# Block-recurrent cross attention and mixture of depths on one core: transfers held behind a fetch of rows, score rows by TensorE, and reads in 32x64 tiles

## The chip, the core and the metric

The kernel runs on one core of a Trainium2 chip. A core has TensorE (PE, with its weight loads, PEld), VectorE (DVE), ScalarE (ACT), GpSimd (POOL) and SyncE (SP), and 16 DMA engines which carry what SP, ACT and POOL issue. Times are microseconds on the device. The time before is 209.79, the median of three runs (207.62 to 210.34).

## What is computed

Two blocks, one after the other, all in float32. The first is attention in both directions between x (8 batches, 8 heads, 512 rows, 64 columns) and a state (32 rows in each head). The second takes from each batch of 544 rows (512 of x, 32 of the state) the 128 with the highest score and sends these through a two-layer network; all other rows pass unchanged.

```python
scores = scale * np.matmul(x, state.transpose(0, 1, 3, 2))     # softmax over the 32 state rows
xread = np.matmul(a, state)
scores2 = scale * np.matmul(state, x.transpose(0, 1, 3, 2))    # softmax over the 512 rows of x
sread = np.matmul(a2, x)
...
scores = np.einsum('bsd,d->bs', x, w_gate)       # x: now (8, 544, 512)
for b in range(B):
    top_idx = np.argpartition(-scores[b], capacity)[:capacity]   # capacity 128
    h = np.maximum(x[b, top_idx] @ w1, 0.0)      # w1: 512 x 1024
    ye = h @ w2                                  # w2: 1024 x 512
    g = 1.0 / (1.0 + np.exp(-scores[b, top_idx]))
    out[b, top_idx] = x[b, top_idx] + g[:, None] * ye
```

## The kernel before

The work is cut into 676 pieces. Each piece belongs to one engine, has a name and a batch, and knows which pieces must come before it. They are numbered as the program makes them, and the list ORDER says in which order they are emitted; each engine then runs its own pieces strictly in that order. In `30/6/w08` the piece is 30, its PSUM bank is 6, and `w08` puts 8 warm-up matmuls (L159) that write bank 0 ahead of it.

A batch runs through these pieces:

- `load_x` (L284): the 1 MB of x of the batch, in two or four transfers. For batches 4 to 7 `load_x2` (L299) brings a second, rearranged copy in four transfers of 256 KB, which VectorE turns in blocks (`blocks`, L395); for batches 0 to 3 TensorE turns x (`turn`, L391).
- `scores` (L428): state against x on TensorE. VectorE makes the softmax over the state in passes over 128 x 1024 elements: `in` (L447), `max` (L458), `sub` (L461), `sum` (L468), `mult` (L473), `out` (L476). ScalarE takes the exponentials. The softmax over x goes by `smax` (L482) and `sexp` (L486).
- `read` (L539): two pieces a batch, on TensorE. The weights are 32 rows of the softmax, 128 columns wide, and the moving operand is the state with one more column, in which the gate is already multiplied in, so that the read leaves the scores of the 512 rows as well (`gate`, L547). With `b in WIDE` a read is 16 matmuls in tiles of 32x128. The rows are copied out by ScalarE (`rows`, L543).
- `sread` (L601): the read of x for the state, on TensorE. Batches 4 to 7 turn its weights through DRAM (`a_out`, L567, and `a_in`, L572).
- `store_x` and `store_s` (L631, L635): all 544 rows of the batch to the output in DRAM, for batches 0 and 1 from ScalarE's queue, for the others from SP's.
- The choice. Each row must be compared with all others, so the 544 scores are laid out as one row on all 128 partitions. Batches 0 to 3 do this on TensorE, by four transposes of a broadcast column and a fifth for the state's rows (`row`, L673, and `row_s`, L676), with two copies by ScalarE. Batches 4 to 7 (`ROWS_OUT`) turn the scores once (`row_t`, L681), write them to DRAM from ScalarE's queue (`row_out`) and read them back on all partitions from SP's (`row_in`, L688). VectorE compares in five windows (`win`, L708), TensorE counts (`over`, L734), VectorE makes a one-hot table (`oh`, L745), TensorE picks row numbers and scores with it (`pick`, L761), and VectorE adds up the row number (`index`, L765).
- `fetch` (L770): GpSimd brings the 128 chosen rows back from the output in DRAM by an indirect transfer. It waits for the stores of its batch.
- The two layers, for the batches in the groups [0], [1, 2], [3, 4], [5, 6], [7]: `xg` (L827) turns the fetched rows, `first` (L868) is 8 pieces, `second` (L888) 4 pieces a batch (or two halves of 4, `second_h`, in batches 6 and 7), then `add` and `put`, which writes the rows back by number.

Five buffers take x and the states, so x of batch 4 takes the place of the states, and x of 5 that of batch 0. There is one buffer for the rearranged copy: x2 of the next batch waits for `blocks` of the last.

Of the kernel before, what the change touches and what calls it, by code (L numbers as in the profile page):

```python
# [18 lines left out]
0 1 4 2 17 3 6 7 8 9 19 30/6/w08 26/5 32/0 10 11 34/4 36/7 18 33 37 12 113/3 5 27 35 31 13 14 38/0 115/6 24/5 117/2 39  # L19
118 25 116 114 15 40/0 28/7 16 44 41 119/5 22 21 23 20 29 45 120 46 42 53 178/2 62/6 180/3 182/5 64/7 184/4 121/0 43  # L20
183 179 65 63 185 267/7 66/5 268 181 67 47 48 126 122 70 49/2 51/4 269/3 50 52 270 127 128 271/4 71/7 174/2 141/6
143/5 175 142 272 144 54/0 176/6 145/4 273/5 123 132 124 55 487 72 125 56 57 146 177 274 129 149 58/0 150/7 328/6
485/4 61 130 151 59 131 73/5 75/7 329 60 68 74 76 486 133/0/w01 137/4 135 136 139 140 69 330 81 78 80 134 77 79 138
186/2 83/4 152/5 154/6 275/0 82 147 148 153 155 191 84 187 85 157 192 193 86/6/w43 206/7 88 280 159 156 158 160 188 89
161 208/3 87 207 209 281 282 210/5/w23 295/4 162/6 163 164 189 297/2 95/6 165/3/w31 296 298 166 96 190 299/7 276 194
167 195 197 196 90 169 97/6 98 102/4 99 103 100 198/0 277 278 104 211 170 101 200 91 201 279 105 286 214 199 202/0
215/6 106 205 204 283 216 203 284 285 333 336 331 332 335 422 423 213 334 488 489 212 587 92 168 226 107/5 217/0 219/2
300 218 220 223 225 221 222 224 108 239/6 287/0 227/4 109 240 289 290 340 337 228 288 229 93 230/7 303 232 291/0 110
304/6 233 94 338 339 292 111 305 231 293 294 424 301 425 171 315 234 112 341/1 241/6 306/5 308/4 342 346 343 242 307
309 347 235 348 236 314 344 361 352 362 426 363 302 427 345 349 312 350 313 351 311 429 431 430 428 252/6 253 243/4  # L30
249/5 246/7 244 353/0 250 247 310 354 245 355 356 254 248 251 364 490 316/4 357/0 365/6 317 172 318 358 359 360 366
492 367 432/4 319/3 369 370/7 433 237 371 321 434 437 261/6 372/0 255/7 262 256 263 257 258 373 374 320 438 439 435
452 173 322 238 323 381 453 493 375 454 368 491 436 455 440 441 376 378 380 379 377 442 382/5 444/0 446 447 495 383
384 445 394/5 385/4 264 448/0 387 259 494 496 443 497 388 589 590 456/7 386 395 450 451 324 457 265 449 460 498/4
396/6 461/3 462 503 463/2 397 464 465 504 505 260 325 389 472 407/7 404/2 401/6 398/3 408 399 405 402 518 519 499 500
501 591 520 466 592 521 458 459 502 390 400 406 403 506 471 507 470 469 467 468 508 473/5 510/0 509 593 474 511 475
522/4 476/5 391 512 513 523 409 326 594 392 478 526 514/0 527/6 410/7 515 595 528 596 516 517 327 479 538 529/4 530
531 597/2 598 602 599 603 604 477 524 532 617 618 600 534 537 535 533 536 525 619 588 601 605 620 411 416/4 412 413
417 539/6 540 541 606 418 542/5 544 608 607 414 551/6 419 609/0 621/7 611 543 612 622 552 545 480 546 610 625 553/5
613/0 626/7 614 627 628/7 547 554 616 629 630 615 481 624 631 623 637 393 548 266 482 636 483 420 632 635 634 633  # L40
558/5 564/6 555/1 561/2 559 562 556 565 557 560 563 638/5 566 639 640 567/4 568 641/5 581/1 569 570 574/7 582 583 643
549 642 421 484 415 550 644 645 646 573 647 650/3 575 576 584 577 651 578 585 571 648 657/5 658 659 652/4 653 654 655
660 579 580 649 586 662 572 669 656 661 663/4/w03 670/2 664 671 665 666 672 673 667 674 668 675
# [4 lines left out]
def kernel(  # L48
# [10 lines left out]
    nc = tc.nc  # L59
# [32 lines left out]
    TURNED = (0,)  # L92
    GATES_PE = (0, 2)
    WIDE = (0, 1, 2, 3, 4, 5, 6, 7)
    ROWS_OUT = (4, 5, 6, 7)
# [177 lines left out]

    def load_x(b, pieces=2):
        buf = xf[b] = Buf(R_X)
        n = H // pieces
        p_x[b] = []
        for h in range(0, H, n):

            on = "ACT" if b == 0 and h + n == H else "SP"  # L280

            def go(h=h, on=on):
                queue = nc.scalar if on == "ACT" else nc.sync
                queue.dma_start(out=buf.ap[:, h:h + n], in_=x[b, h:h + n].rearrange("h (p c) d -> p h c d", c=NC))  # L284

            chain = [q for q in last_load if q.engine == on][-1:]
            p_x[b].append(add(on, "load_x", go, after=chain, takes=[] if h else [buf], uses=[buf] if h else [], b=b))
            last_load.append(p_x[b][-1])

    def load_x2(b):  # L290

        buf = x2[b] = Buf(R_X2)
        p_x2[b] = []
        for w in range(2):
            for e in range(2):
                def go(w=w, e=e):
                    src = x[b].rearrange("h (s t r w) (e d) -> w e t r h s d", s=4, t=32, r=2, e=2)[w, e]
                    o = 32 * (2 * w + e)
                    nc.sync.dma_start(out=buf.ap[o:o + 32], in_=src)  # L299

                p_x2[b].append(add("SP", "load_x2", go, after=[p_scores[b - 2]], takes=[] if p_x2[b] else [buf], uses=[buf] if p_x2[b] else [], b=b))
# [316 lines left out]
    def touches(b, st, by_number=False):  # L618
        for bb, others in touch.items():
            if bb != b:  # L620
                for s, n in others:
                    if n or by_number:
                        tc.declare_no_dep(st.ins, s.ins, reason="rows of another batch")
        touch.setdefault(b, []).append((st, by_number))

    def store_base(b, xs, tmp, p_xs, p_xt):
        on = "ACT" if b < 2 else "SP"
        queue = nc.scalar if on == "ACT" else nc.sync

        def x_rows():  # L630
            touches(b, queue.dma_start(out=out[b, 0:S].rearrange("(p c) m -> p c m", c=NC), in_=xs.ap))  # L631

        def s_rows():
            dst = out[b, S:SP].rearrange("n (g q d) -> q n g d", g=2, q=4)
            touches(b, queue.dma_start(out=dst, in_=tmp["xt"]))  # L635

        return [add(on, "store_x", x_rows, after=p_xs, uses=[xs], b=b), add(on, "store_s", s_rows, after=[p_xt], b=b)]

    def by_number(b, **kw):

        touches(b, nc.gpsimd.indirect_dma_start(**kw), True)  # L641
        nc.gpsimd.memset(z1, 0.0)

# [3 lines left out]
    def choice(b, tmp, p_sc, p_xt, p_st1):  # L647
# [105 lines left out]
        for lo, hi in slot_tiles:  # L753
# [16 lines left out]
            def fetch(m=m, u=u, xr=xr):  # L770
                by_number(b, out=xr.ap[0:m], out_offset=None, in_=flat_out[0:SP * (b + 1)],
                          in_offset=bass.IndirectOffsetOnAxis(ap=u["idx"].ap[0:m, 0:1], axis=0))
# [31 lines left out]
            u["got"] = add("POOL", "fetch", fetch, after=[p] + p_st1, takes=[xr], uses=[u["idx"]], b=b)  # L804
            q = add("POOL", "below", below, after=[q], takes=[u["z"]], uses=[u["ax"]], b=b)
# [159 lines left out]
```

## Time and profile before

| | |
|---|---|
| median of three runs | 209.79 |
| the profiled execution's own time | 207.89 |
| its span, first to last instruction | 206.1 |
| mean granted TensorE clock | 0.963 |
| DMA | 36.14 MB, mean 175 GB/s |
| fetches of rows, issued at | 40.99, 58.54, 69.25, 95.28, 110.24, 133.39, 149.48, 174.53 |
| issue to landing of the eight, least, median, most | 3.3, 3.9, 5.6 |
| last matmul starts, last put starts | 198.7, 202.10 |

A group of instructions in the timeline is a start, a duration, an engine, a line, what is written from what, and a count; in square brackets stands the idle time ahead of it and what ended it. A matmul of float32 appears as two instructions. The chain of waits is the work that ended last, followed back from the end. A row by window gives the busy time of PE, PEld, DVE, ACT and POOL, then the granted clock (1.00 is full), the busy share of the DMA engines and what they moved.

### The profile page before, as it was taken

The page shows a single profiled execution, that of the slowest core. Times are in us where ns is not written, and L with a number is a line of the kernel's source. Part 1 is how long each engine was busy: PE and PEld are TensorE (multiplying, and loading weights), DVE is VectorE, ACT ScalarE, POOL GpSimd, SP SyncE. Part 2 cuts the span into 40 slices and gives each one's busy share as a digit, 9 for nine tenths or more (in the row PEclk, how much of TensorE's full clock was granted, in tenths as well). Part 3 has the DMA queues.
Part 4 walks back from the last instruction along what each step waited for, and adds up shares of the span by engine and source line. Part 5 has one row for each costly group of instructions (what it writes and reads, how often), then busy time and mean ns, then how long its engine had stood idle before and what let it go on. Part 6 is the DMA issues. An engine that isn't in the chain of part 4 may idle for free.

```text
span 206.1 us, 5307 instructions
## 1 busy us (share of the span) xinstructions
PE 192.1 (93%) x2204; PEld 141.5 (69%) x2204; DVE 125.6 (61%) x293; ACT 75.7 (37%) x174; POOL 49.3 (24%) x147
## 2 busy tenths in 40 slices
PE   7999997979999999999989999999999999999960
PEld 3786775558976568884456788844578885699840
DVE  2379896696959699848988579769940511011010
ACT  2399984463274252163305522524052040010200
POOL 7030010071032260014304300120064231305222
PEclk9999997596999999999999999999999999999995
DMA  6999999992399199988586999465833520100200
GB/s 194 362 305 391 356 219 268 371 244 98 52 264 310 50 285 243 149 113 261 142 167 122 148 233 171 177 256 169 177 84 106 220 102 0 51 3 26 76 25 25
DMA packets 67832, 36.14 MB, mean 175 GB/s; under 512 B 54988, under 2 KB 63200, under 8 KB 66784
## 3 DMA queue, kind: packets, MB, share of 16 engines
q1 hardware_dynamic: 64848, 28.97, 54.7%
q0 software_dynamic: 1312, 4.20, 6.6%
q10 hardware_dynamic: 1648, 2.63, 3.7%
q8 instruction: 17, 0.28, 0.6%
q14 instruction: 7, 0.06, 0.1%
HBM read 22.68 MB, written 13.12 MB: 174 GB/s over the span
## 4 chain that ended last, share of the span: by engine, by line
PE 70%; DMA 12%; issue 5%; DVE 5%; ACT 4%; SPq 1%; POOLq 1%; POOL 0%; DVEq 0%
PE ps L868 28%; PE ps L888 18%; PE ps L539 7%; DMA xr<-out_dram,idx 5%; PE ps L428 4%; PE ps L601 3%; DMA xf<-in_x_dram 3%; PE ps L827 2%; DMA row_d<-row_t 2%; PE ps L734 2%; PE ps L391 2%; DMA x<-in_x_dram 1%; DMA out_dram<-ot,half 1%; ACT xT L408 1%; DVE eT L476 1%
## 5 line engine op out<-in xcount | busy, mean ns | idle before, releaser
L888 PE MATMUL ps<-w,hT 128*128 128x512 f32 (+1 forms) x160 | 58.6, 514 | 0.0
L868 PE MATMUL ps<-xg,w 128*128 128x256 f32 (+1 forms) x320 | 58.1, 342 | 0.1
L868 PEld LDWEIGHTS ps<-xg,w 128*128 128x128 f32 x320 | 51.4, 194 | 5.5 <-ACT xg L830 0.4
L888 PEld LDWEIGHTS ps<-w,hT 128*128 128x128 f32 x160 | 29.3, 190 | 19.8 <-issue 18.0
L543 ACT COPY xs<-ps 128x512 f32<-128x512 f32 x32 | 17.5, 592 | 27.8 <-PE ps L539 20.5
L708 DVE SCALAR_TENSOR_TENSOR win<-srow,sc,after 32x32 bf16<-32x32 f32 (+4 forms) x40 | 18.4, 500 | 7.0 <-DMA srow<-row_d 7.0
L891 DVE SCALAR_TENSOR_TENSOR ot<-ps,z,xr 128x512 f32<-128x512 f32 (+1 forms) x10 | 6.2, 633 | 26.3 <-PE ps L888 23.4
L871 ACT ACTIVATE hT<-ps 128x512 f32<-128x512 f32 x16 | 9.2, 603 | 34.2 <-PE ps L868 34.2
L641 POOL DMA_INDIRECT xr<-out_dram,idx x8 | 8.5, 1066 | 45.9 <-DVE idx L765 21.2
L539 PE MATMUL ps<-st_v,eT 32*128 32x65 f32 x512 | 18.0, 276 | 1.3 <-issue 0.5
L539 PEld LDWEIGHTS ps<-st_v,eT 32*128 32x128 f32 x512 | 15.8, 186 | 4.9 <-DVE eT L476 1.9
L468 DVE TENSOR_REDUCE sm<-e 128x32 f32<-128x1024 f32 x8 | 9.7, 1213 | 4.0 <-ACT e L464 3.9
L486 ACT ACTIVATE a<-ps,nm 128x512 f32<-128x512 f32 x14 | 9.5, 686 | 5.0 <-DMA row_d<-row_t 3.9
L464 ACT ACTIVATE e<-e 128x1024 f32<-128x1024 f32 x8 | 8.5, 1066 | 7.2 <-DVE e L461 7.2
L395 DVE STREAM_TRANSPOSE xT<-x 128x512 f32<-128x512 f32 x16 | 10.5, 684 | 1.0 <-DMA x<-in_x_dram 1.0
L391 PE MATMUL ps<-ident,xf 128*128 128x128 f32 x64 | 9.9, 289 | 0.7 <-ACT eT L516 0.3
L428 PE MATMUL ps<-xT,st_T 64*32 64x256 f32 x256 | 10.1, 429 | 0.5 <-DVE sc L547 0.5
L447 DVE STREAM_TRANSPOSE e<-ps 128x1024 f32<-128x1024 f32 x7 | 8.7, 1238 | 2.3 <-PE ps L428 2.3
L473 DVE TENSOR_TENSOR e<-e,sm 128x1024 f32<-128x1024 f32 x8 | 9.8, 1221 | 0.1
L601 PE MATMUL ps<-xf,aT 128*32 128x64 f32 x512 | 9.6, 232 | 0.0
L797 POOL TENSOR_TENSOR z<-z 128x1 f32<-128x1 f32 x8 | 2.3, 291 | 30.0 <-DVE z L793 21.3
L391 PEld LDWEIGHTS ps<-ident,xf 128*128 128x128 f32 x64 | 7.6, 149 | 2.7 <-issue 0.9
(110 smaller groups left out, 232.1 us busy)
## 6 DMA issues: line engine op xcount, KB each, us to landing
xf<-in_x_dram SPq DMA_DIRECT2D x14, 512.0 KB, 5.9
out_dram<-xs SPq DMA_DIRECT2D x6, 1024.0 KB, 5.7
w<-in_moe_w_dram SPq DMA_DIRECT2D x2, 2048.0 KB
x<-in_x_dram SPq DMA_DIRECT2D x16, 256.0 KB, 5.3
out_dram<-xs ACTq DMA_DIRECT2D x2, 1024.0 KB
a_d<-spare SPq DMA_DIRECT2D x4, 512.0 KB
aT<-a_d SPq DMA_DIRECT2D x16, 128.0 KB, 2.9
srow<-row_d SPq DMA_DIRECT2D x4, 272.0 KB
```

Source lines behind the costliest of these rows:

```text
L391: nc.tensor.transpose(v[:, k, r], xf[b].ap[:, 2 * pair + k, 2 * r:2 * r + 2].rearrange("p w d -> p (w d)"), ident)
L395: nc.vector.transpose(out=t.ap.rearrange("p k r t -> p r k t"), in_=x2[b].ap[:, :, 2 * pair:2 * pair + 2].rearrange("p r k s d -> p r k (s ...
L428: nc.tensor.matmul(view_s(False)[Ns * q:Ns * (q + 1), w, g], st_T[half, b, g, Ns * q:Ns * (q + 1)], xT[2 * g + q // 2].ap[half, q % 2].rea ...
L468: nc.vector.reduce_sum(out=sm, in_=e.ap, axis=AX.X)
L473: nc.vector.tensor_tensor(out=e.ap, in0=e.ap, in1=tmp["sm"].to_broadcast([128, 32, Ns]), op=ALU.mult)
L486: nc.scalar.activation(out=a.ap[:, g], in_=view_s()[:, :, g], func=AF.Exp, bias=tmp["nm"][:, g:g + 1], accum_out=tmp["ss"][:, g:g + 1])
L539: nc.tensor.matmul(view(o)[t, q, c - c0, g], eT.ap[r, c % 2, g, c // 2, t], st_v[r, b, g], start=True, stop=True)
L543: nc.scalar.copy(out=xs.ap[:, c].rearrange("p (g q m) -> p g q m", g=2, q=4), in_=view(o)[:, :, c - c0, :, 0:D].rearrange("p q g m -> p g ...
L601: nc.tensor.matmul(o2.ap[rr, D * g:D * (g + 1)], (aT[g].ap if aT else aT2.ap[:, g])[:, c, rr], xf[b].ap[:, 4 * g + q, c], start=(c == 0), ...
L708: nc.vector.scalar_tensor_tensor(wins[c].ap[0:n], srow.ap[0:n, f:SP], sc[0:n, b, c:c + 1], after[0:n, 0:SP - f], op0=ALU.is_gt, op1=ALU.mu ...
L868: nc.tensor.matmul(o, w(j), i[:, :, j] if n == 256 else i[:, 0, j], start=(j == 0), stop=(j == ND - 1))
L888: nc.tensor.matmul(py.ap[0:m, part], hT.ap[:, f, lo:lo + m], w2[:, f, part], start=(f == 0), stop=(f == NF - 1))
```

## The change

Four parts.

1. A load of x or x2 of batches 4, 5, 6 and 7 waits for the landing of the fetch of batch 0, 2, 3 and 4, and the two stores of batch 1 for that of batch 0. These stores also go from ScalarE's queue to SP's. SP's queue runs in order, so what is emitted behind a held transfer waits with it.
2. Batches 4 to 7 lay out their scores on TensorE, as 0 to 3 do: `row`, `row_kept`, `row_s`, `row_s_kept` in place of `row_t`, `row_t_kept`, `row_out`, `row_in`. The number of pieces is the same.
3. The reads of batches 4 to 7 go in tiles of 32x64, 32 matmuls a read in place of 16.
4. ORDER is another one, with other banks and other places for the warm-up matmuls.

```diff
+    HELD = {4: 0, 5: 2, 6: 3, 7: 4}
+    HELD_ST = {1: 0}
     GATES_PE = (0, 2)
-    WIDE = (0, 1, 2, 3, 4, 5, 6, 7)
-    ROWS_OUT = (4, 5, 6, 7)
+    WIDE = (0, 1, 2, 3)
+    ROWS_OUT = ()
...
+    fetched = {}
+
+    def behind(b, st):
+
+        for p in fetched.get(b, ()):
+            tc.add_manual_dep(st.ins, p.ins.name, mybir.DependencyInfo(mybir.DependencyClass.Sync, mybir.DependencyReason.DATA),
+                              reason="transfers behind the fetch of rows")
...
-                queue.dma_start(out=buf.ap[:, h:h + n], in_=x[b, h:h + n].rearrange("h (p c) d -> p h c d", c=NC))
+                behind(HELD.get(b), queue.dma_start(out=buf.ap[:, h:h + n], in_=x[b, h:h + n].rearrange("h (p c) d -> p h c d", c=NC)))
...
-                    nc.sync.dma_start(out=buf.ap[o:o + 32], in_=src)
+                    behind(HELD.get(b), nc.sync.dma_start(out=buf.ap[o:o + 32], in_=src))
...
-                    if n or by_number:
+                    if (n or by_number) and s.ins not in [p.ins for p in fetched.get(HELD_ST.get(b), ())]:
...
-        on = "ACT" if b < 2 else "SP"
+        on = "ACT" if b < 1 else "SP"
...
+        def store(st):
+            touches(b, st)
+            behind(HELD_ST.get(b), st)
...
+            fetched.setdefault(b, []).append(u["got"])
```

The two orders, decoded into names of pieces (`.1` is the batch or, for the layers, the group; `x3` is three of the same; `w3` is three warm-up matmuls). VectorE, up to the index of batch 0:

```
before: twice.0 numbers turned.0 x2 smax.0 max.0 sub.0 ssum.0 sum.0 mult.0 smax.1 in.1 gate_s.0 max.1 ssum.1 sub.1 gate.0
        gates.6 score_s.0 sum.1 gate_s.1 mult.1 score_s.1 gate.0 out.1 gates.4 win.0 x3 gate.1 win.0 x2 gate.1 smax.2 off.0
        in.2 oh.0 win.1 index.0 smax.3 win.1 x4 max.2 off.1
after:  twice.0 numbers turned.0 x2 smax.0 max.0 sub.0 ssum.0 gates.6 sum.0 mult.0 in.1 smax.1 max.1 sub.1 gate_s.0 ssum.1
        score_s.0 gate.0 gates.4 sum.1 gate.0 mult.1 out.1 win.0 x4 in.2 win.0 gate.1 smax.2 max.2 gate_s.1 gate.1 smax.3
        off.0 score_s.1 oh.0 sub.2 index.0 in.3 win.1 x5 ssum.2 sum.2 max.3 off.1
```

TensorE, from the row of batch 0 to the end of group 1:

```
before: row.0 row_s.0 w1 read.1 x2 scores.2 over.0 row.1 row_s.1 scores.3 w3 pick.0 turn_a.2 x2 w3 sread.2 turn_a.3 over.1
        turn_a.3 xg.0 w1 pick.1 sread.3 first.0 x6 read.2 first.0 x2 read.2 heads.2 second.0 row.2 row_s.2 second.0 xg.1
        read.3 over.2 second.0 pick.2 read.3 second.0 heads.3 scores.4 xg.1 row.3 row_s.3 first.1 x6 read.4 first.1 x2
        over.3 read.4 sread.4 scores.5 pick.3 heads.4 second.1 row_t.4 second.1 x6 over.4 read.5 xg.2 pick.4 second.1
after:  row.0 row_s.0 w2 scores.2 state_T.6 read.1 sread.1 read.1 scores.3 over.0 heads.1 w1 turn_a.2 row.1 turn_a.2 pick.0
        row_s.1 w1 state_T.4 sread.2 turn_a.3 x2 over.1 xg.0 w3 first.0 x5 pick.1 read.2 first.0 x2 heads.2 read.2 first.0
        row.2 row_s.2 second.0 xg.1 read.3 over.2 second.0 pick.2 read.3 sread.3 second.0 row.3 heads.3 scores.4 row_s.3
        xg.1 second.0 first.1 over.3 first.1 x2 pick.3 first.1 x5 read.4 xg.2 sread.4 read.4 heads.4 row.4 row_s.4
        second.1 x2 over.4 scores.5 second.1 x2 pick.4 second.1 x4
```

SP, behind the loads of x 0 to 3, states and weights:

```
before: load_x2.4 x2 load_x.4 x2 load_x2.4 load_x.5 x2 store_s.2 load_x2.4 load_x.6 x2 store_x.2 load_x.7 load_x2.5
        store_x.3 load_x2.5 x2 a_out.4 store_s.3 load_x2.5 a_in.4 load_x2.6 x2 store_x.4 load_x2.6 row_in.4 a_out.5
        store_s.4 load_x2.6 a_in.5 load_x2.7 x3 a_out.6 row_in.5 load_x2.7 a_in.6 store_x.5 store_s.5 store_x.6 row_in.6
        store_s.6 a_out.7 load_x.7 a_in.7 store_s.7 row_in.7 store_x.7
after:  store_x.1 store_s.1 load_x2.4 load_x.4 load_x2.4 x2 store_s.2 load_x2.4 store_x.2 load_x.4 store_x.3 store_s.3
        load_x2.5 load_x.5 load_x2.5 a_out.4 load_x2.5 x2 a_in.4 load_x.5 load_x2.6 x3 store_s.4 load_x2.6 store_x.4
        load_x.6 a_out.5 a_in.5 load_x2.7 x3 a_out.6 load_x2.7 load_x.6 a_in.6 store_x.5 store_s.5 load_x.7 store_s.6
        store_x.6 load_x.7 a_out.7 a_in.7 store_x.7 store_s.7
```

From the first piece of the first layer to the end, the pieces `first` and `second` stand on TensorE in 20 unbroken stretches before and in 26 after.

## The prediction

> **What bounds the kernel now.** I read the page's busy shares first, then the busy rows of the 40 slices, then the chain of waits around the first fetch of rows, then windows laid on the places where the PE rows show less than full.
>
> ```profile
> PE 192.1 (93%) x2204; PEld 141.5 (69%) x2204; DVE 125.6 (61%) x293; ACT 75.7 (37%) x174; POOL 49.3 (24%) x147
> PE   7999997979999999999989999999999999999960
> PEclk9999997596999999999999999999999999999995
> DMA  6999999992399199988586999465833520100200
> ```
>
> TensorE is the bound: 192.1 of 206.1 us. The holes are at the start, in slices 5 to 9 (26 to 51 us), and in the last slice; there the granted clock falls too.
>
> ```profile
> 30.60:34.00 3.40, 2.37 (x80) 1.97 (x84) 2.04 (x9) 2.48 (x7) 0.00 (x0) 1.00 0.97 309
> 34.00:37.40 3.40, 3.40 (x58) 1.94 (x50) 2.95 (x9) 0.80 (x3) 0.00 (x0) 0.50 1.07 229
> ...
> 44.20:47.60 3.40, 1.67 (x18) 1.29 (x17) 3.26 (x6) 1.00 (x2) 1.33 (x4) 1.00 0.98 298
> 47.60:51.00 3.40, 3.40 (x76) 3.20 (x72) 1.88 (x4) 1.61 (x3) 1.01 (x5) 0.50 0.10 32
> 49.67:199.10 149.43, 147.78 (x1425) 109.13 (x1425) 90.39 (x216) 42.99 (x102) 35.25 (x105) 1.00 0.59 143
> ```
>
> (Window, its length, busy PE, PEld, DVE, ACT, POOL, then clock, DMA share, GB/s.) From 49.67, the first matmul of the first layer, to 199.1 PE idles 149.43 - 147.78 = 1.65 us in all. So what comes after 49.67 can shrink only by less PE work; before it, waits and half clock are to be had. The chain there:
>
> ```profile
> 40.53 0.17 DVE idx L765
> 40.70 0.30 issue
> 40.99 5.63 DMA xr<-out_dram,idx
> 46.63 0.14 issue
> 46.76 0.63 PE ps L827 x4
> 47.39 0.21 PE ps L159
> 47.61 0.20 PE ps L761 x5
> 47.80 1.86 PE ps L601 x64
> 49.67 6.23 PE ps L868 x48
> ```
>
> The fetch of batch 0 takes 5.63 us; over the eight fetches the landing is 3.3 at least, 3.9 in the median, 5.6 at most. The longest is the one under a DMA share of 1.0 (the weights, x of batches 4 and 5, the store of batch 1).
>
> **The change part by part,** against this execution: 207.89 us, a span of 206.1 and 1.79 around it. The median of the runs shown, 209.79, lies 1.9 above it.
>
> *The holds.* Store 1 and x of batch 4 now come after fetch 0. Until then the queues carry x 0 to 3, states, weights and store 0, about 10 MB; before, the slices to 46 us moved 14 MB at about 300 GB/s. 10 MB are through at about 34 us, so fetch 0 should run in a quiet queue: 3.3 us for 5.63 (ends: 2.4, the shortest landing of any transfer by row number, to 5.63, if the time is not contention). I take 3.3.
>
> *When it is issued.* VectorE sets that. Before, it ended the division of batch 0 (mult) at 18.9. In the new order the state gates of batch 6 (0.8) come ahead of it and use up the 0.54 us wait before the sum: 19.15. From there to the row numbers of batch 0 the order lists, by the durations of the timeline: nine passes over 1024 columns at 1.2 (in, smax, max, sub of 1; in, smax, max, sub of 2; smax of 3) 10.8; the sum of 1 with its reciprocal 1.7; mult and out of 1 2.35; five windows 2.5; gates 0.8; one-hot 0.75; small ones 2.0. Together 20.9, so the index is there at 40.1 and the fetch goes at 40.4, beside 40.99. That is with VectorE never waiting; each wait is a delay. It lands at 43.7. But the counting of batch 1 (over) now stands ahead of the turn of the rows: in of 3 (1.2) and five windows (2.5) after 40.1 make 43.8, then 0.6 of over and 0.5 of turn, 0.6 of copy: the first layer starts at 45.8 at best.
>
> *The clock.* The Trainium skill, "TensorE: Matmul & The Clock Gate" (What's actually happening), has half clock after an idle window of about 3.4 us. By it nothing should dip here: no PE gap is near 3.4. The rows say otherwise: half clock follows the windows in which PE was busy 2.37 and 1.67 of 3.4. The new order puts some 14 us of PE work in the 17 us from 30 to 47, 2.8 per 3.4, between these and full. By the page the start is 45.8; by the trace one dip costs up to 1.7. I take half a dip: 46.6. So the first layer starts **3.1 earlier** (0 to 3.9).
>
> *Work moved behind that start*: the state read of batch 3 (1.03 at full clock) and the pick of batch 1 (0.2): **+1.2**. The half clock from 49.67 to 51 cost 0.65, which is in the start's half dip now: **-0.65**.
>
> *Score rows on TensorE, batches 4 to 7.*
>
> ```profile
> 61.88 0.60 PE L673 MATMUL ps<-ident,sc 128*128 128x128 f32 x4
> 62.41 0.24 PE L676 MATMUL ps<-ident,sc 32*128 32x32 f32 x1
> ...
> 95.67 0.27 PE L681 MATMUL ps<-ident,sc 128*5 128x128 f32 x1
> ```
>
> On the chain four transposes take 0.44 and the fifth 0.17; the removed one took 0.12 to 0.27, mean 0.19. So +0.42 x 4 = **+1.7**. ScalarE gains copies of 0.59 and 0.19 for one of 0.26, +0.5 x 4, beside 37% busy: nothing. The rows' two transfers go, with VectorE's 7.0 us of waits for them and two issues per batch (0.33 on SP). PE waited 0.48 before L681 in all: **-0.5**. The rest had been covered by the first and second layer, so the eight microseconds between a row's turn and its landing are not won.
>
> *Reads in 32x64, batches 4 to 7*: 64 instructions for 32, in eight groups. The trace has none in this shape.
>
> ```profile
> 24.42 0.43 PE L359 MATMUL ps<-wg_T,st_T 64*32 64x1 f32 x32
> ...
> 111.19 1.12 PE L539 MATMUL ps<-st_v,eT 32*128 32x65 f32 x32
> 112.24 1.10 PE L601 MATMUL ps<-xf,aT 128*32 128x64 f32 x64
> ```
>
> Start to start, group less one instruction's duration: L539 (1.12 - 0.27)/31 = 27.4 ns, L601 (1.10 - 0.22)/63 = 14.0, L359 (0.43 - 0.17)/31 = 8.5. The same page says (Wait — 56ns, not 53.3ns?) that start to start never drops below about 25 ns, which speaks against this change: 63 x 25 + 270 = 1.85 us a group, +5.8 for eight. The trace has 14.0 and 8.5, so the floor does not hold here. Half the weight columns should halve the 27.4, to about L601's 14.0 (1.15 a group, +0.3 in all); eight tiles in place of four, as L359 has, allow 8.5 (0.81, -2.5). I take 11 between the two nearest rows: 0.96 a group, **-1.3**; ends -2.5 and +7.0 (no gain per instruction).
>
> *The new order.* Behind the start, the layers' matmuls stood in 20 unbroken stretches; in the new order there are 26. A stretch of 4 at 512 columns took 1.91 where 20 took 8.78 (1.76 per 4), and 64 first-layer matmuls broken in 48 + 16 took 14.28 beside 13.82 and 14.08: 0.15 to 0.45 a break. 6 x 0.2 = **+1.2** (0 to 2.7). Warm-up matmuls: 17 for 16 before the start, 3 and 3 behind it: nothing.
>
> *What queues behind the held transfers.* The two stores of batch 1 leave ScalarE's queue (issues of 0.36 and 0.64, at 34.3, while ScalarE waits: nothing won) for SP's. SP's queue stands from about 14 us to the landing of fetch 0: store 1, then x of 4. Before, x2 of 4 was wanted by VectorE at 65.8; issued from 44 and landing in 5.3 (at most 8.3), it is ready by 55. Fetch 1 waits for store 1: issued 44, landing 5.7, near 50; its pick stands behind five of the eight pieces of the first layer (46.6 + 5.2). x of 5 behind fetch 2, of 7 behind fetch 4 have like slack. x of 6 behind fetch 3 has the least: by the old times 95.28 + 3.9, four issues at 1.1, 5.3 to land: 108.9, against a first use at 107.3; the new order has the pick of 3 ahead of five of the eight first-layer pieces of group 1, before behind all. Cost taken: 0. SP also loses the rows' waits for their DRAM trip. The tail after the last matmul, about 7 us, is untouched: the last two puts follow each other as before.
>
> Sum: -3.1 + 1.2 - 0.65 + 1.7 - 0.5 - 1.3 + 1.2 = -1.45; 207.89 - 1.45 = **206.4 us**.
>
> **The rivals.**
> - *More is won*: no dip (-0.8), reads at 8.5 ns (-1.2), the other 1.15 of PE idle behind the start gone: 203.3; without the price of breaks 202. For it: the dips are the largest loss in the profile, and a fetch with free queues may vary less. Against: VectorE has no slack before 40 us.
> - *Slower*: the 32x64 reads start no faster than 27.4 ns. Place: eight reads, all on the bound engine. Then +7.0 in place of -1.3: 214.7 (25 ns: 213.5). It decides from 13.9 ns on, where the sum is the old time, and shows as slower by 2% from 26 ns. Against it: L601 and L359.
> - *A wash*: the fetch lands late for another reason, or a dip falls on the first layer (start 48 to 49), and rows and breaks eat the rest: 208.5.
> - *A held load is late*: x of 6 by 3 to 5 us with VectorE waiting, then PE before the scores of 6: 210 to 212. Layer work of some 7 us can be in front of it, so I give it little.
> - That the holds do nothing is not possible for batch 4 and store 1, which stood ahead of fetch 0 before.
>
> **How the numbers follow.** The sum 0.40 (204.5 to 208.5), more is won 0.32, a wash 0.14, slow reads 0.10, late load 0.04. Two per cent, about what a measurement of this kernel can tell from no change, is 205.6 and 214.0 around 209.79. Under 205.6: nearly all of "more is won" and three tenths of the sum, 0.42. Above 214.0: most of the slow reads, 0.08. Between: 0.50. The range 202 to 211 leaves out the slow reads and the best part of the second case; faster and no change hold most of the chance, and the sum's own range stands above.
>
> **What would show it.** Right: fetch 0 issued at 40 to 41 and landing in under 4 us; the first layer starting at 46 to 47; 64 read instructions in about 1.0 us; some 0.6 us of row turns per batch; PE without holes behind the start. Wrong: half clock on the first layer; reads near 2 us; VectorE waiting for x2, or SP waiting long for a fetch while PE idles.

## The result, and the profile after

The changed kernel takes 206.34 us, the median of 20 runs (204.99 to 208.99). Before, beside it, 20 runs have a median of 209.86 (207.27 to 211.59). The ratio is 0.987, with an interval of 0.984 to 0.991: faster by a little over one per cent, which is less than the two per cent that were to be told from no change. Medians here are over all runs, while a ratio compares only runs within 1.5 per cent of the fastest of their kernel. The profiled execution took 205.92, with a span of 204.1; that of before took 207.89, with a span of 206.1.

The page of the kernel after, with the shares and the 40 slices:

```profile
PE 189.9 (93%) x2477; PEld 139.5 (68%) x2477; DVE 126.6 (62%) x293; ACT 77.4 (38%) x178; POOL 55.3 (27%) x147
PE   7799898879899999999999999899999999999990
PEclk9999999999999999999999999999999999999999
DMA  6999945019996799799979969787750062102200
```

TensorE is still the bound, at the same share. The dips of the PEclk row are gone. The DMA row falls to 0 and 1 in slices 7 and 8 (36 to 46 us), where it stood at 9: in front of the first fetch the queues are empty. Windows of the kernel after (start and end, length, busy PE, PEld, DVE, ACT, POOL, clock, DMA share, GB/s):

```profile
34.00:40.80 6.80, 6.05 (x109) 4.55 (x110) 6.80 (x13) 5.17 (x14) 2.25 (x4) 1.00 0.08 17
44.20:47.60 3.40, 2.43 (x17) 1.81 (x18) 3.33 (x8) 1.50 (x4) 0.20 (x1) 1.00 0.57 234
47.60:51.00 3.40, 3.40 (x33) 3.40 (x32) 3.09 (x5) 0.00 (x0) 0.00 (x0) 1.00 0.89 189
46.47:198.76 152.29, 150.33 (x1766) 110.54 (x1766) 89.10 (x211) 45.28 (x108) 41.24 (x111) 1.00 0.69 159
```

The DMA share ahead of the fetch is 0.08, and the clock is full in all four windows. The last row runs from the first matmul of the first layer to the end of the last matmul. PE idles 152.29 - 150.33 = 1.96 us in it. The start itself, in the timeline of the kernel after:

```profile
39.69 0.15 DVE L782 TENSOR_REDUCE idx<-ps 128x1 int32<-128x2 f32 x1
39.76 1.24 DVE L457 STREAM_TRANSPOSE e<-ps 128x1024 f32<-128x1024 f32 x1
41.10 1.68 POOL L656 DMA_INDIRECT xr<-out_dram,idx  x1 [0.70 <-DVE e L457]
45.14 0.66 PE L845 MATMUL ps<-ident,xr 128*128 128x128 f32 x4 [1.38 <-DMA xr<-out_dram,idx]
45.17 0.37 SPq L645 DMA_DIRECT2D out_dram<-xs  x1
46.47 4.73 PE L886 MATMUL ps<-xg,w 128*128 128x128 f32 x40
```

The row numbers are there at 39.84, the fetch is issued at 41.10, its rows are turned at 45.14, the held store of batch 1 leaves at 45.17, and the first layer starts at 46.47. From issue to turn it is 4.04 us; before it was 5.77.

Between the row numbers and the fetch lie 1.26 us, where before had 0.30. GpSimd has small pieces to do until 40.39 and then stands idle for 0.70. The profile puts this idle time down to VectorE's pass L457 (`in` of batch 3), which the new order places right behind the row numbers: it ends at 41.00, and the fetch goes out 0.10 later. The fetch uses nothing that this pass writes. In all seven kernels with the new order the idle time is 0.70 or 0.71 and the distance from the end of that pass 0.09 or 0.10; why the fetch waits for it was not tested.

The holds moved traffic and did not remove it. Fetch 0 lands in 4.0 us for 5.6, but fetches 1, 2 and 3 take 5.1, 5.6 and 5.4, for 4.7, 3.8 and 5.1 before. PE waits for none of these three in after.

The other end, in the timelines of the last second layer, first of before and then of after (L891 and L909 are `add_h`, L641 and L656 `put`):

```profile
192.01 7.07 PE L888 MATMUL ps<-w,hT 128*128 128x256 f32 x32
197.54 0.48 DVE L891 SCALAR_TENSOR_TENSOR ot<-ps,z,xr 128x256 f32<-128x256 f32 x1 [11.46 <-PE ps L888]
198.80 1.00 POOL L641 DMA_INDIRECT out_dram<-ot,half  x1 [7.03 <-issue]
202.10 0.96 POOL L641 DMA_INDIRECT out_dram<-ot,half  x1 [2.18 <-DMA out_dram<-ot,half]
```

```profile
191.69 7.07 PE L906 MATMUL ps<-w,hT 128*128 128x256 f32 x32
196.21 0.48 DVE L909 SCALAR_TENSOR_TENSOR ot<-ps,z,xr 128x256 f32<-128x256 f32 x1 [9.81 <-PE ps L906]
196.97 0.96 POOL L656 DMA_INDIRECT out_dram<-ot,half  x1 [7.12 <-DVE ot L909]
198.80 0.48 DVE L909 SCALAR_TENSOR_TENSOR ot<-ps,z,xr 128x256 f32<-128x256 f32 x1 [2.11 <-PE ps L906]
200.14 0.96 POOL L656 DMA_INDIRECT out_dram<-ot,half  x1 [2.09 <-DVE ot L909]
```

From the first of these matmuls the first half's rows are added after 4.52 us instead of 5.53, and put after 5.28 instead of 6.79. The second put comes 3.30 after the first in before and 3.17 in after.

So the two executions differ in three stretches:

| stretch | before | after | difference |
|---|---|---|---|
| to the first matmul of the first layer | 49.67 | 46.47 | -3.20 |
| from there to the end of the last matmul | 149.43 | 152.29 | +2.86 |
| from there to the end of the span | 7.0 | 5.34 | -1.65 |
| the execution's own time | 207.89 | 205.92 | -1.97 |

The medians differ by 3.5, which is 1.5 more. The profiled execution of before happened to be one of its quick ones (2.0 below its median), that of after less so (0.4 below). Part of what varies from one execution to the next goes with the granted clock. In three sets of executions of before (64, 27 and 27, beside the experiments) a straight line through times and clocks falls by 0.9, 1.05 and 1.25 us for each 0.01 of clock, with a wide scatter (correlations of -0.57, -0.66 and -0.76). The median clock is 0.968 to 0.969 before and 0.991 after, and by these lines the 0.022 between them would be some 1.9 to 2.7 us. The quickest execution of before in any set, 204.36, is as quick as the quickest of after, 204.99. So what the change brings in the median goes with rarer stretches at half clock. This is a correlation over executions, not an experiment, and the clock is not all: the profiled execution of before was quick at a clock of 0.963, under the median clock. What made it quick is not known.

### The profile page after: what moved, and what is told of

Read it like the earlier page. It is cut to its first block, busy times and chain, and to the rows that moved or that the text cites. A ratio compares the mean times of both kernels' runs of the same rounds, so it can differ in the third digit from the quotient of the medians.

```text
span 204.1 us, 5849 instructions
## 1 busy us (share of the span) xinstructions
PE 189.9 (93%) x2477; PEld 139.5 (68%) x2477; DVE 126.6 (62%) x293; ACT 77.4 (38%) x178; POOL 55.3 (27%) x147
## 5 line engine op out<-in xcount | busy, mean ns | idle before, releaser
L886 PE MATMUL ps<-xg,w 128*128 128x256 f32 (+1 forms) x320 | 59.2, 341 | 0.0
L886 PEld LDWEIGHTS ps<-xg,w 128*128 128x128 f32 x320 | 50.5, 191 | 7.3 <-issue 1.4
L725 DVE SCALAR_TENSOR_TENSOR win<-srow,sc,after 128x544 bf16<-128x544 f32 (+4 forms) x40 | 18.2, 504 | 7.7 <-ACT srow L716 7.7
L909 DVE SCALAR_TENSOR_TENSOR ot<-ps,z,xr 128x512 f32<-128x512 f32 (+1 forms) x10 | 6.1, 628 | 22.5 <-PE ps L906 18.7
L549 PE MATMUL ps<-st_v,eT 32*64 32x65 f32 (+1 forms) x768 | 16.9, 246 | 2.0 <-DVE sc L557 0.7
L735 POOL CAST aux<-sc 128x5 bf16<-128x5 f32 x8 | 3.0, 378 | 57.5 <-DVE sc L679 23.9
L656 POOL DMA_INDIRECT xr<-out_dram,idx x8 | 9.6, 1194 | 30.9 <-DVE idx L782 13.4
L549 PEld LDWEIGHTS ps<-st_v,eT 32*64 32x64 f32 (+1 forms) x768 | 14.6, 149 | 4.3 <-issue 2.1
L557 DVE TENSOR_REDUCE sc<-ps 128x2 f32<-128x16 f32 x16 | 2.7, 170 | 14.5 <-PE ps L549 8.2
L405 DVE STREAM_TRANSPOSE xT<-x 128x512 f32<-128x512 f32 x16 | 10.6, 688 | 0.0
L611 PEld LDWEIGHTS ps<-xf,aT 128*32 128x32 f32 x512 | 7.9, 110 | 2.7 <-issue 1.6
L848 ACT COPY xg<-ps 128x512 f32<-128x512 f32 x8 | 4.6, 594 | 13.0 <-PE ps L845 13.0
```

The source lines that it names most:

```text
L405: nc.vector.transpose(out=t.ap.rearrange("p k r t -> p r k t"), in_=x2[b].ap[:, :, 2 * pair:2 * pair + 2].rearrange("p r k s d -> p r k (s ...
L549: nc.tensor.matmul(view(o)[t, q, c - c0, g], eT.ap[r, c % 2, g, c // 2, t], st_v[r, b, g], start=True, stop=True)
L611: nc.tensor.matmul(o2.ap[rr, D * g:D * (g + 1)], (aT[g].ap if aT else aT2.ap[:, g])[:, c, rr], xf[b].ap[:, 4 * g + q, c], start=(c == 0), ...
L656: st = nc.gpsimd.indirect_dma_start(**kw)
L725: nc.vector.scalar_tensor_tensor(wins[c].ap[0:n], srow.ap[0:n, f:SP], sc[0:n, b, c:c + 1], after[0:n, 0:SP - f], op0=ALU.is_gt, op1=ALU.mu ...
L886: nc.tensor.matmul(o, w(j), i[:, :, j] if n == 256 else i[:, 0, j], start=(j == 0), stop=(j == ND - 1))
```

## The experiments

Each kernel stands with the median of before that was taken beside it. Where that is 208.75, the ratio rests on only two of before's 27 runs (the fastest is 204.36), so for these four kernels I read the medians and the profiles and not the ratio. Intervals are 95 per cent.

| kernel | median us (runs) | before beside it | ratio, interval |
|---|---|---|---|
| after, no holds | 208.28 (22) | 210.15 | 0.997 [0.994, 1.000] |
| after, all reads in 32x128 | 207.16 (14) | 210.15 | 0.989 [0.985, 0.993] |
| after, old order of the last halves | 208.06 (22) | 210.15 | 0.994 [0.991, 0.998] |
| after, all reads in 32x64 | 210.74 (19) | 210.15 | 0.998 [0.995, 1.002] |
| before, new order of the last halves | 209.50 (22) | 208.75 | 1.001 [0.990, 1.012] |
| before, rows on TensorE | 228.02 (6) | 208.75 | 1.111 [1.097, 1.125] |
| before, reads of 4 to 7 in 32x64 | 209.84 (6) | 208.75 | 1.021 [1.008, 1.034] |
| before, more warm-ups at 34 us | 210.16 (6) | 208.75 | 1.021 [1.007, 1.035] |
| before with the holds | 220.31 (6) | 209.46 | 1.063 [1.055, 1.070] |
| before, rows on TensorE, second copy early | 224.42 (6) | 209.46 | 1.079 [1.071, 1.087] |
| after, rows through DRAM | 245.49 (6) | 209.46 | 1.182 [1.175, 1.188] |
| after, store 3 held too | 207.56 (22) | 209.46 | 0.995 [0.992, 0.998] |

### The holds: taken away from after

```diff
-    HELD = {4: 0, 5: 2, 6: 3, 7: 4}
-    HELD_ST = {1: 0}
+    HELD = {}
+    HELD_ST = {}
```

> The changed kernel without its waits: no load and no store waits for a fetch of rows, order and everything else as changed. Theory that the holds pay: fetch 0 runs beside x of batch 4 and store 1 and lands in 5 us or more, where it took 3.9, the first layer starts 1 to 2 us later than 46.5, and the ratio to the kernel before goes from 0.987 to 0.992 to 0.997. Rival, that the new order alone brings the gain: first layer at 46 to 47, ratio 0.985 to 0.990. Second rival, that the holds cost something further on: ratio under 0.984.

208.28, ratio 0.997 where after has 0.987; the intervals are apart. Its timeline:

```profile
40.37 1.68 POOL L656 DMA_INDIRECT xr<-out_dram,idx  x1 [0.70 <-DVE e L457]
45.94 0.88 PE L845 MATMUL ps<-ident,xr 128*128 128x128 f32 x4 [2.90 <-DMA xr<-out_dram,idx]
47.90 5.47 PE L886 MATMUL ps<-xg,w 128*128 128x128 f32 x40
```

The fetch is issued 0.73 earlier than in after and its rows are turned 0.80 later: 5.57 us from issue to turn, for 4.04. PE waits 2.90 there, the clock drops (0.77 from 45.9 to 53.4; 40 matmuls of the first layer take 5.47 for 4.73), and the layer starts 1.43 later. The order is the same, so in this order the holds are worth about 1 per cent, as the theory said. The three other parts without them leave 0.3 per cent, with an interval that reaches up to no gain: that the new order brings it all is not so.

### The holds alone, in the old order

The waits and SP's queue for the stores of batch 1 were put into before. Its ORDER was kept, but for x of batch 4 and the stores of batch 1, which were moved to right behind fetch 0, and x and x2 of 5, 6 and 7, behind fetches 2, 3 and 4.

```diff
+    HELD = {4: 0, 5: 2, 6: 3, 7: 4}
+    HELD_ST = {1: 0}
     WIDE = (0, 1, 2, 3, 4, 5, 6, 7)
     ROWS_OUT = (4, 5, 6, 7)
```

> The kernel before with the first part of the change alone: x of batches 4 to 7 and the stores of batch 1 wait for the fetches, their pieces stand right behind these in the order, everything else as before (rows through DRAM, all reads 32x128, the old order and tail). Theory that the quiet queue for fetch 0 is the gain, because a shorter wait of TensorE also spares it the half clock at the start of the first layer: fetch 0 lands in under 4.2 us, median clock over 0.98, median 1.5 to 3 us under the kernel before. Rival, that the new order is needed to use it: 0 to 1 us less, clock as before (0.97). Rival, that late loads cost as much: no change or slower.

220.31: slower by 6 per cent, which only the last rival left room for. The timeline of the start (L632 is the fetch, L821 the turn of the rows, L862 the first layer):

```profile
38.07 1.23 POOL L632 DMA_INDIRECT xr<-out_dram,idx  x1 [7.95 <-DVE idx L758]
41.86 0.65 PE L821 MATMUL ps<-ident,xr 128*128 128x128 f32 x4
44.04 5.62 PE L862 MATMUL ps<-xg,w 128*128 128x128 f32 x48
```

The start is the best of all kernels: 3.79 us from issue to turn, the first layer at 44.04, 5.63 before that of before, with no half clock. Of the 5.63 the fetch is 2.0, and 2.9 are an earlier issue. Then it is lost. Behind the start, up to the last matmul, PE idles 13.4 us where before idles 1.65, and it is busy 5.7 us longer, at a clock of 0.95. A later part of the same timeline (SPq is SP's queue, with the time that the issue took):

```profile
79.57 0.75 SPq L285 DMA_DIRECT2D x<-in_x_dram  x1
85.24 2.49 DVE L381 STREAM_TRANSPOSE xT<-x 128x512 f32<-128x512 f32 x4 [6.77 <-DMA x<-in_x_dram]
101.83 5.32 SPq L285 DMA_DIRECT2D x<-in_x_dram  x3
107.27 1.67 SPq L681 DMA_DIRECT2D srow<-row_d  x1
112.55 0.78 DVE L701 SCALAR_TENSOR_TENSOR win<-srow,sc,after 128x544 bf16<-128x544 f32 x1 [7.84 <-DMA srow<-row_d]
113.40 0.21 PE L727 MATMUL ps<-ones,win 128*128 128x1 bf16 x2 [5.21 <-DVE win L701]
```

The score row of batch 4 comes back from DRAM on SP's queue and stands there behind the held x2 of batch 6 (L285). It leaves at 107.27, for 100.11 in before. VectorE waits 7.84 us for it, and PE 5.21 for VectorE. Before that VectorE had waited 6.77 for x2 of batch 5, and PE 5.02 for VectorE. There the hold itself is not what is late: the first quarter of this x2 leaves at 67.59, earlier than in before (70.21), but the last one stands in the queue behind a store and other transfers and leaves at 79.57, for 80.31 in before. So VectorE turns it at 85.24, for 85.44, and the head start is gone by then. The rival of the prediction, a held load that is late, is real in the old order in this form: what stands behind a held load in SP's queue is late. In after the score rows don't go through SP, and no wait of VectorE for x or x2 is in its profile. A version that holds only x of 4 and store 1 in the old order was not tried.

### Rows through DRAM, in after

```diff
-    ROWS_OUT = ()
+    ROWS_OUT = (4, 5, 6, 7)
```

The four pieces of a row and its windows then stand where the second copy of the row stood.

> The changed kernel with the score rows of batches 4 to 7 through DRAM again, each group of its pieces where the second transpose stood in the new order. Theory: TensorE has 1.7 us less to do, but the new order leaves no room for the 8 us of the way, so windows, counts and picks come late and TensorE waits: slower by 3 us or more than the changed kernel (206.3). Rival, that the order has slack enough: 204.5 to 206.

245.49: slower, as the theory said, but by 39 us and not 3. The waits of PE in it:

```profile
PE ps L727 <- DVE win L701: 23.1, 6, 7.6
```

(Total, times, longest.) Six waits for the comparing windows, of up to 7.6 us, are the trip through DRAM in the open, as the count now follows close behind the turn. The 39 us are the price of the trip in an order that leaves no room for it, not of the trip as such: in before, where the order has the room, VectorE waits 7.0 us for the rows in all.

### Rows on TensorE, in before

```diff
-    ROWS_OUT = (4, 5, 6, 7)
+    ROWS_OUT = ()
```

> The kernel before with the score rows of batches 4 to 7 by TensorE, order unchanged. Theory of the sum: 1.7 us more of TensorE, at most 0.5 us of waits saved, ratio 1.004 to 1.008. Rival, that the way through DRAM held up VectorE and the fetches, and its end pays more than the transposes cost: ratio 0.990 to 0.998.

228.02, far outside what both said. Waits of PE in it:

```profile
PE ps L734 <- DVE win L708: 7.7, 2, 6.5
PE ps L888 <- ACT srow L699: 2.4, 1, 2.4
```

In the old places the row's second copy (L699) stands late in ScalarE's queue, and PE waits for it here and, for 1.2, ahead of the first layer; for the comparing windows it waits 7.7. So the copy was moved up, to right behind its matmul:

> The kernel before with the score rows of batches 4 to 7 by TensorE, and here the second copy of the row follows its transpose at once on ScalarE, in place of standing where the load from DRAM stood in the order (as it did in the run with 228 us). Theory of the sum: 1.7 us more of TensorE less 0.5 of waits, median 1 to 2 us over the kernel before. Rival, that the shorter way pays more than it costs: median 1 us or more under it.

224.42, and the expectation was missed again. PE's waits for the copy fall from 3.6 to 0.6 us, about what the median gained; the 7.7 for the windows stay. Its timeline (L864 is the second layer, L652 the state's part of the row):

```profile
96.78 0.60 PE L649 MATMUL ps<-ident,sc 128*128 128x128 f32 x4
97.22 10.46 PE L864 MATMUL ps<-w,hT 128*128 128x512 f32 x24
107.61 0.24 PE L652 MATMUL ps<-ident,sc 32*128 32x32 f32 x1
```

Six pieces of the second layer, 10.46 us, stand between the two parts of one row. Both kernels say that a piece's place costs far more than the piece: the matmuls added are 0.60 and 0.24. Neither isolates the cost of the rows in the time; that is read from the durations in after.

### The shape of the reads

```diff
-    WIDE = (0, 1, 2, 3)
+    WIDE = (0, 1, 2, 3, 4, 5, 6, 7)
```

> The changed kernel with all reads in 32x128 tiles. Theory that the reads lie on the bound engine: eight reads at 1.05 us of TensorE in place of 0.85, so 1.6 us more, ratio to before 0.994 to 0.996. Rival, that the reads of batches 4 to 7 are hidden behind VectorE: ratio stays at 0.985 to 0.989.

207.16 against 206.34, with overlapping intervals: 0.8 is not resolved, and the ratio, 0.989, is the one that the rival named. The profile resolves the group: 0.92 us in after for a read of batches 4 to 7, for 1.12 in before.

```profile
88.04 0.92 PE L549 MATMUL ps<-st_v,eT 32*64 32x65 f32 x64
```

Behind the start, PE is busy 152.13 with 32x128 and 150.33 with 32x64. Of these 1.8 some 1.1 are not the reads: in that execution fetch 2 came late and a second layer's piece behind it ran at half clock (2.98 for 1.88). The saving is read from the groups, eight by 0.2, and is not shown in the time. The other way, all reads in 32x64:

```diff
-    WIDE = (0, 1, 2, 3)
+    WIDE = ()
```

> The changed kernel with the reads of batches 0 to 3 in 32x64 tiles as well. Theory: 0.2 us less of TensorE for each of the eight reads; four of them (batches 2 and 3) lie behind the start of the first layer, where TensorE has no holes, so 0.8 us less and a ratio of 0.982 to 0.985; the reads of batches 0 and 1 lie where VectorE sets the time and give nothing. Rival, that every read counts: 1.6 us less, ratio 0.979 to 0.981. Rival, [...]a dip of the granted clock before 47 us, ratio 0.990 or more.

210.74. The quicker reads of batches 0 to 3 bring no time and cost about 1 per cent against after; the dip and the ratio of the last rival came. Its profiled execution is one of the longer ones (211.49, where its runs go from 206.89 to 212.90). The page's PEclk row and windows of it:

```profile
PEclk9999999797999999999999999999999999999996
```

```profile
32.00:36.00 4.00, 1.07 (x60) 0.81 (x56) 3.21 (x6) 1.31 (x4) 0.00 (x0) 0.96 0.34 117
36.00:40.00 4.00, 4.00 (x116) 2.51 (x109) 1.44 (x4) 2.80 (x8) 0.00 (x0) 0.61 0.02 6
```

```profile
31.48 1.08 PE L611 MATMUL ps<-xf,aT 128*32 128x64 f32 x59
35.50 0.31 PE L611 MATMUL ps<-xf,aT 128*32 128x64 f32 x5 [2.93 <-issue]
```

PE is busy for 1.07 of 4 us, and the clock of the next four is 0.61. The fetch is issued at 43.69 and the first layer starts at 49.16. In after PE is busy for 3.28 of the first of these windows, and the clock stays full. But the reads ahead of the window are only 0.2 us shorter each. Most of the hole is one gap of 2.93 in the middle of the state read of batch 1, for which the profile names nothing that PE waits for. So the dip follows a gap, and that the shorter reads made the gap is not shown. Over all runs the median clock is 0.984, for 0.991 in after.

In before, with the reads of batches 4 to 7 in the changed shape:

```diff
-    WIDE = (0, 1, 2, 3, 4, 5, 6, 7)
+    WIDE = (0, 1, 2, 3)
```

> The kernel before with the reads of batches 4 to 7 in 32x64 tiles, order unchanged. Theory of the sum: eight reads of 0.85 us of TensorE in place of 1.05, 1.6 us less, ratio 0.991 to 0.994. Rival, from the run with all reads wide, which lost only 0.4 us: ratio 0.996 to 1.000. A read group near 2 us[...]: ratio above 1.02.

209.84 with 208.75 beside it: no gain that shows, and the ratio forecast was missed. A group takes 0.92 here as well, so the size holds in both orders; 1.6 us (eight groups by 0.2) would be small beside the spread of these runs (208.97 to 212.40, and 204.36 to 211.61 in before).

### The order of the last two halves

The last second layer has two halves of 256 columns, with four pieces each. Before, they alternate (1 2 1 2 1 1 2 2 by half); after has 1 1 1 2 1 2 2 2, so the first half is complete one piece, 0.88 us, earlier.

```diff
-663/4/w23 664 665 670/6 666 671 672 673
+663/4/w23 670/6 664 671 665 666 672 673
```

> The changed kernel with the second layer of the last group in the order of the kernel before: its two halves interleaved, so that the first half is complete after six of eight pieces and not after five. Theory that the tail made part of the gain: the put of the second half waits again for the landing of the first, the time from the last matmul to the end goes from 5.3 to about 7 us, ratio to before from 0.987 to 0.993 to 0.996. Rival, that the shorter tail is chance of one execution: tail 5 to 6 us, ratio 0.985 to 0.989.

208.06, ratio 0.994. Its timeline at the end:

```profile
193.85 7.07 PE L906 MATMUL ps<-w,hT 128*128 128x256 f32 x32
199.23 0.48 DVE L909 SCALAR_TENSOR_TENSOR ot<-ps,z,xr 128x256 f32<-128x256 f32 x1 [10.66 <-PE ps L906]
199.99 0.96 POOL L656 DMA_INDIRECT out_dram<-ot,half  x1 [7.97 <-DVE ot L909]
203.15 0.96 POOL L656 DMA_INDIRECT out_dram<-ot,half  x1 [2.09 <-issue]
```

From the first matmul to the second put it is 9.30 us, for 8.45 in after: 0.85 by the order of the halves. From the last matmul to the end it is 6.3 us, between the 7 of the theory and the 5.3 of after. The rest of the 1.7 in the medians is not explained by it. In before it is 10.09 to the second put, 0.79 more again, of which 0.50 lies between the first add's end and the first put (0.78 for 0.28). The converse, in before:

```diff
-663/4/w03 670/2 664 671 665 666 672 673
+663/4/w03 664 665 670/2 666 671 672 673
```

> The kernel before with one thing of the change: the pieces of the last group's second layer in the new order, first half complete after five of eight pieces. Theory that the tail is a gain of its own: ratio 0.992 to 0.995 (1.0 to 1.6 us less), last matmul to end 5.3 to 6 us. Rival, that it only paid together with the rest: ratio 0.998 to 1.002.

From the first matmul to the end of the span it is 13.21 us for 14.09, so 0.88 by the profile. In the time nothing shows: 209.50 with 208.75 beside it, where the runs spread over 8 us. From the first add's end to the first put it is 0.77 here. So the half microsecond there goes with the old order (0.78 and 0.77) and not with the order of the halves: both kernels with the new one have 0.28. In the old order GpSimd's `halved` stands right ahead of this put, in the new one it is done earlier; whether that is the reason was not tested.

### More warm-up matmuls at 34 us, in before

```diff
-137/4 135 136 139 140
+137/4/w42 135 136 139 140
...
-275/0 82
+275/0/w02 82
```

> The kernel before with two warm-up matmuls more ahead of the second read of batch 1 and two more ahead of the scores of batch 2, where TensorE stood idle for 0.5 us each before the clock fell. Theory that half clock is a loss of its own: no half clock from 34 to 41 us, the index of batch 0 up to 2 us earlier, ratio 0.990 to 0.995. Rival, that VectorE and the fetch set this stretch: the warm-ups bring nothing or cost their own 0.4 to 1.5 us, ratio 1.000 to 1.006.

210.16 with 208.75 beside it: no gain, as the rival said. A window and the timeline of this kernel:

```profile
34.00:40.80 6.80, 6.42 (x132) 4.10 (x123) 6.27 (x15) 4.28 (x12) 1.74 (x3) 1.00 0.99 272
```

```profile
39.06 1.23 POOL L641 DMA_INDIRECT xr<-out_dram,idx  x1 [9.14 <-DVE idx L765]
46.30 1.09 PE L827 MATMUL ps<-ident,xr 128*128 128x128 f32 x4 [3.36 <-DMA xr<-out_dram,idx]
49.81 6.36 PE L868 MATMUL ps<-xg,w 128*128 128x128 f32 x44
```

The half clock at 34 to 37 is gone and the fetch is issued 1.93 earlier than before, but its rows are turned at 46.30 (before 46.76): 7.24 us for the fetch, under a DMA share of 0.99 up to its issue and 0.93 behind it. The first layer starts at 49.81. In this execution an earlier issue and a full clock bring nothing, as the fetch lands no earlier: what limits this start is the transfers ahead of the fetch.

### Store 3 held behind fetch 2 as well

```diff
-    HELD_ST = {1: 0}
+    HELD_ST = {1: 0, 3: 2}
```

> The changed kernel with one hold more: the stores of batch 3 wait for fetch 2, beside which they run in the changed kernel (fetch 2 goes at 65.2, store 3 at 66.5, and the turn of its rows is due at 70.6). Theory that a fetch beside a store of 1 MB is slow by 1.5 to 2 us and makes TensorE wait in some executions: fetch 2 lands in under 4.5 us, median 0.3 to 1.5 us under 206.3 and the highest runs under 208. Rival, that fetch 2 is hidden or the later store delays fetch 3: median within 0.3 of 206.3 or above.

207.56, median 1.2 above that of after, as the rival said. In its timeline fetch 2 goes out and has landed when the store leaves:

```profile
64.47 1.06 POOL L656 DMA_INDIRECT xr<-out_dram,idx  x1 [6.41 <-DVE z L810]
68.42 0.36 SPq L645 DMA_DIRECT2D out_dram<-xs  x1
70.09 0.66 PE L845 MATMUL ps<-ident,xr 128*128 128x128 f32 x4
```

It lands in 3.9 us, for 5.6 in after, as the theory said, and brings nothing: PE turns these rows at 70.09 straight behind the piece before, and in after (70.82) it did so too. Fetch 2 lies beside other work, though with nothing to spare: with all reads in 32x128 PE waited 2.72 for it.

### What the fetch takes, over all kernels

From the issue of fetch 0 to the turn of its rows, by the timelines: with x of 4 and store 1 held 3.79, 4.03, 4.04, 4.08, 4.10, 4.13 and 4.14; not held 5.44, 5.57, 5.77, 5.79, 6.29, 6.49 and 7.24. The two sets don't overlap, whatever the order, the shape of the reads or the place of the rows.

## Why the prediction was right

The forecast was 206.4 and the time is 206.34. So near a hit is luck in two ways. The sum was made against one profiled execution, 207.89, which lay about 2 us under the median: from the 209.79 of the three runs the same sum would say 208.3. And within the profiled executions, where it said -1.45 and -1.97 came, two misses cancel: +1.2 behind the start and -1.65 in the tail. What was right is the mechanism of the start, and that the work behind it grows.

- **The start, -3.1: right, at -3.20, by a path that was in part another.** The row numbers came at 39.84 for 40.1. The fetch was issued at 41.10 for 40.4: the 0.70 behind VectorE's pass was not in the forecast. It landed in 4.0 us where I had 3.3. I had the counting of batch 1 as the last thing ahead of the turn; in fact it was done at 43.77, and PE waited 1.38 for the fetch. Against these delays stand two things in the forecast. I charged half a dip of the clock, 0.8, and none came in this execution. And my sum for the start was 0.3 too long: 43.8 with 0.6, 0.5 and 0.6 is 45.5, not 45.8. That the transfers made the fetch slow is shown by taking the holds away, and by the two sets above.
- **Behind the start.** I had +1.65 (all terms but the start, with -0.65 for half clock among them), and it is +2.86. Rows: four transposes and the fifth take 0.53 and 0.17 without overlap, less 0.18 for the one removed, +2.1 over four batches for 1.7. Reads: 0.92 a group for 0.96, or 0.85 net of what overlaps its neighbours for 1.05, so -1.6 for -1.3. The state read and the pick moved as said. PE's idle time, from which I took 0.5, grew by 0.3. What is left for the breaks between layers is about 1.5 for 1.2; it is the remainder, not measured alone.
- **The floor of 25 ns** that the prediction quotes. (0.92 - 0.25)/63 is 10.6 ns from start to start, so the measurement decides against it for these tiles. The slow reads, which rested on 25 ns or more, are refuted; the estimate of 11 between L601 and L359 was right.
- **The step that failed** is "the tail after the last matmul, about 7 us, is untouched: the last two puts follow each other as before". It shrank by 1.65. The second put does follow the first as before, by 3.2, but this is why the first sets the end, and the new order completes the first half a piece earlier. 0.85 to 0.88 of it is shown by the two kernels with exchanged halves; 0.5 lies between add and put, goes with the rest of the new order, and is unexplained.
- **Held loads.** Lateness 0 in after, as said. That this depends on the order and on the rows leaving SP's queue was not in my text; the holds alone, at 1.063, show what a queue behind held loads costs where they don't.
- **More is won, with a fetch that varies less:** its price in one execution, 203.3, wasn't reached. Its remark fits what the medians show, a higher clock in the median execution, but no kernel isolates it. The kernel without holds has a median clock of 0.986, and the 0.005 to after's 0.991 would be only some 0.5 of the 1.9 us between them.

## What to carry to other kernels

Holding bulk transfers back until a small, urgent fetch has landed paid here where the bound engine waits for that fetch (fetch 0, not fetch 2), and only where nothing urgent stood in the queue behind what is held. Before switching one part of such a change on or off, ask where its pieces stand in each engine's order: the holds, the rows on TensorE and the rows through DRAM, each switched alone, made kernels 6 to 18 per cent slower, though the whole brings 1. Of two writes of which the second waits for the first, the first sets the end, so its input should be finished first. And a forecast that is summed against one execution should be compared with that execution, and not with a median.

## What the runs showed of the hardware

- The clock fell to half after windows in which PE was busy 2.37 or 1.67 of 3.4 us (before) or 1.07 of 4 (all reads in 32x64), not only after an idle one; after 2.43 of 3.4, in the changed kernel, it stayed full. Where the line lies can't be told from these.
- A wait costs twice: 64 matmuls of the state read took 1.10 us at full clock and 1.94 after the wait for the fetch (before, and before with more warm-ups); 40 of the first layer took 4.73 and, after the wait of 2.90 without holds, 5.47.
- An indirect fetch of 128 rows takes 3.8 to 4.1 us from issue to use beside nearly empty queues and 5.4 to 7.2 beside full ones. Two puts of which the second waits for the first are 3.2 to 3.3 apart.
- Between the row numbers and the first fetch lie 0.30 us in four kernels with the old order and 1.7 to 3.3 in the three others; with the new order it goes out 0.1 after a VectorE pass ends, in all seven. The reason is open.
- Issuing the first fetch occupied GpSimd for 1.68 us in the changed program, and 1.23 in before's with the holds or the warm-ups; fetch 2 took 1.06.
- Matmuls of float32 in tiles of 32x64, 65 columns each, started every 10.6 ns, for 27.4 in tiles of 32x128 (mean over a group of 64 and of 32).
